# The sums of squares of v fetched through the weights' raw buffers, and split buffers shared by the halves of a lone token block

## The chip, the cores and the metric

The kernel runs on one core of one Trainium2 chip. The core has five engines with a queue each: TensorE (PE in the rows; its weight loads PEld), VectorE (DVE), ScalarE (ACT), GpSimd (POOL) and SyncE (SP), which only issues transfers. DMAs are issued by SyncE, ScalarE and GpSimd and run on the core's 16 DMA engines. The metric is the device time of one execution in microseconds; of several executions the median is told.

## The reference

Three stages on a batch of 4 sequences of 576 tokens. Causal attention with 8 heads of 64 and a decay made from `f`:

```python
log_f = np.log(np.clip(f, 0.0001, 1.0))
cum = np.cumsum(log_f, axis=-1)
decay = cum[:, :, :, None] - cum[:, :, None, :]
scores = np.where(causal, -1000000000.0, scores + decay)
...
return np.matmul(attn, v).astype(np.float32)
```

then a layer norm and an MLP with a residual (512 to 2048 to 512), and a gated layer in which half of the hidden values `v` are normalised and mixed along the sequence by a 576 x 576 matrix:

```python
ch = np.maximum(xn @ w_ch1, 0.0) @ w_ch2
return (x + ch).astype(np.float32)
...
v_s = np.einsum('ts,bsd->btd', w_spatial, v_n) + b_spatial[None, :, None]
gated = u * v_s
return (gated @ w_out).astype(np.float32)
```

## The kernel before, in words

Tokens are handled in nine blocks of 256 columns (`BLOCKS`): blocks 0 and 1 hold the first 128 tokens of two sequences each, 2 and 3 the next 128, 4 to 7 the rest of one sequence each, and block 8 the last 64 tokens of all four. A block first runs through attention (`attention32`, `attention1` or `attention`, by its kind), then the norm, and then the MLP. The MLP takes blocks in groups (`GROUPS`): group 0 is blocks 0 and 1, groups 1 to 5 are one block each (2 to 6), group 6 is blocks 7 and 8.

The work of attention and of the MLP is interleaved by a table of event times in `run`: each event makes one step of a generator issue its instructions, and a scheduling layer then places the instructions in the engines' queues. An engine works off its own queue strictly in order. While group 0 runs through the MLP, the raw 64-bit weights are still fetched, 1 MB for each of 16 slices of the hidden layer, into two `raw` buffers (L474, L475), made into a high and a low single-precision part on ScalarE and VectorE (`narrow`, L463 to L490), and the low part of the second matrix is stored for later groups (L491). At the same time blocks 2 and 3 run through `attention1`.

Attention of blocks 4 to 7 multiplies `v` in two half-precision parts scaled by a power of two, which comes from the sum of squares of `v` in a sequence. `vnorm` makes these sums: it fetches `v`, five times 1 MB (L210, L213), and squares it on ScalarE with an accumulated sum (L211 for four tiles of 128 x 2048, L215 for the last tile in four pieces); one small matmul adds the partitions (L217). Its event time `VN` is 1.6, behind the first part of block 3's attention, and it uses one `vraw` buffer of its own.

The MLP of a group (`mlp`) first splits the normalised block into a high and a low part: for each of four slices of 128 features ScalarE copies `xh` (L543) and VectorE subtracts `xl` (L544). The tiles are 512 columns wide, for two blocks; a lone block uses the first half. There are four buffers of each name. For each of 16 slices j of the hidden layer follow the first layer (12 matmuls into `ph`), `hh` and `hl` on ScalarE and VectorE (L582, L583), and, one slice later, the second layer of slice j - 1 (12 matmuls into `acc`). So between the making of `hh` and the second layer that reads it stand the second layer of the slice before and the first layer of the next. At the end of a group VectorE multiplies the accumulators by the norm's factor into `t` (L598), of which there are three buffers, and GpSimd issues stores of `t` that add to the residual in memory (L600). Group 0 has eight such evictions, a lone block four. L511 is the square in the norm of a block; L380 and L418 are the products of probabilities and `v`; L372 and L281 are the DMA transposes of the probabilities.

Of the kernel before, what the change touches and what calls it, by code (L numbers as in the profile page):

```python
# [6 lines left out]
F32 = mybir.dt.float32  # L7
F32R = mybir.dt.float32r
# [10 lines left out]
P = 128  # L19
B, H, S, D = 4, 8, 576, 64  # L20
DM, DFF, DF2 = 512, 2048, 1024
NK = DM // P
# [3 lines left out]
TOK = 256  # L26
# [7 lines left out]
MB = dict(xT=3, xh=4, hh=2, wl=2, y=2, t=3)  # L34
# [3 lines left out]
RAWB, TMPB, LOB = 2, 2, 4  # L38
# [6 lines left out]
RAMP = 1.5  # L45
# [5 lines left out]
    SPAN.append((SPAN[-1][1], SPAN[-1][1] + (2.25 - E0 - 0.2) / 4))  # L51
SPAN.append((SPAN[-1][1], SPAN[-1][1] + 0.05))
RAWAT = (-1.1, -1.1)
CLEAD, VN = 3, RAMP + 0.1

ORDER = (2, 3, 4, 7, 0, 1, 5, 6)
M2A, M2S = 0.1, 30
# [10 lines left out]
def f32(ap):  # L68
    return ap.bitcast(F32)
# [7 lines left out]
class Kernel:  # L77
# [123 lines left out]

    def vnorm(self):

        nc, at = self.nc, self.at
        ss = self.cst.tile([P, B, 2], F32, name="vss")
        self.vsc = self.cst.tile([P, 2, B], F32, name="vsc")
        for b in range(B + 1):
            t = at.tile([P, 4, DM], F32, tag="vraw", name="vraw", bufs=1)
            if b < B:
                nc.sync.dma_start(out=t, in_=self.v[b, :512].rearrange("(t p) d -> p t d", p=P))  # L210
                nc.scalar.activation(t, t, AF.Square, accum_out=ss[:, b, 0:1])  # L211
            else:
                nc.sync.dma_start(out=t, in_=self.v[:, 512:].rearrange("b p d -> p b d"))  # L213
                for i in range(B):
                    nc.scalar.activation(t[:, i], t[:, i], AF.Square, accum_out=ss[:, i, 1:2])  # L215
        pn = self.bank("s")
        nc.tensor.matmul(pn[:, : 2 * B], lhsT=self.ones, rhs=ss.rearrange("p b u -> p (b u)"), start=True, stop=True)  # L217
        nc.vector.tensor_reduce(out=ss[:, :, 0], in_=pn[:, : 2 * B].rearrange("p (b u) -> p b u", u=2), axis=mybir.AxisListType.X, op=ALU.add)
        self.pow2(ss[:, :, 0], self.vsc)
# [312 lines left out]
    def mlp(self, g, states, y):  # L532
        nc, mo = self.nc, self.mo
        n = len(states)
        xn = [[mo.tile([P, 2 * TOK], F32R, tag=tag, name=tag, bufs=MB["xh"]) for tag in ("xh", "xl")] for _ in range(NK)]

        def split(i):

            x, c = states[i](), slice(i * TOK, (i + 1) * TOK)
            for t, (xh, xl) in enumerate(xn):  # L540
                scale = self.gT[:, t : t + 1]
                with self.tc.high_priority(1):
                    nc.scalar.activation(xh[:, c], x[:, t, :], AF.Copy, scale=scale)  # L543
                    nc.vector.scalar_tensor_tensor(out=xl[:, c], in0=x[:, t, :], scalar=scale, in1=f32(xh[:, c]), op0=ALU.mult, op1=ALU.subtract)  # L544

        acc = self.accs(n * TOK)
        clear, seen = {}, set()

        def second(j, c, hh, hl, wl, last):
            for m in range(NK):  # L550

                bank = m if n > 1 else m // 2
                first = self.mm3(acc[m][:, c], self.wh[:, j, DM + m * P : DM + (m + 1) * P], wl[:, m * P : (m + 1) * P], hh, hl, bank not in clear, last, skip_group_check=True)
                if bank not in clear:
                    clear[bank] = first
                elif (m, c.start, c.stop) not in seen:
                    self.after(first, clear[bank])
                seen.add((m, c.start, c.stop))

        todo = [(j, 0, n) for j in range(NF)]  # L560
        if g == 0:

            todo = [(j, 0, 1) for j in range(SKEW)] + todo[SKEW:] + [(j, 1, 2) for j in range(SKEW)]
        pend, there = None, 0
        for step, (j, i0, i1) in enumerate(todo):
            while there < i1:
                split(there)
                there += 1
            c, W = slice(i0 * TOK, i1 * TOK), (i1 - i0) * TOK
            if g == 0 and i0 == 0:  # L570
                wl = self.w2lo[j]
            else:
                wl = mo.tile([P, DM], F32R, tag="w2l", name="wl", bufs=MB["wl"])
                nc.scalar.dma_start(out=f32(wl), in_=self.w2l_d[j * P : (j + 1) * P, :])
            ph = self.bank("ph")[:, :W]
            for k in range(NK):
                ks = slice(k * P, (k + 1) * P)
                self.mm3(ph, self.wh[:, j, ks], self.w1l[:, j, ks], xn[k][0][:, c], xn[k][1][:, c], k == 0, k == NK - 1)
            hh = mo.tile([P, 2 * TOK], F32R, tag="hh", name="hh", bufs=MB["hh"])[:, :W]
            hl = mo.tile([P, 2 * TOK], F32R, tag="hl", name="hl", bufs=MB["hh"])[:, :W]  # L580
            with self.tc.high_priority(1):
                nc.scalar.activation(hh, ph, AF.Relu)  # L582
                nc.vector.scalar_tensor_tensor(out=hl, in0=ph, scalar=0.0, in1=f32(hh), op0=ALU.max, op1=ALU.subtract)  # L583
            if pend is not None:
                second(*pend)
            pend = (j, c, hh, hl, wl, step == len(todo) - 1)
            yield
        second(*pend)
        c = GROUPS[g][0] * TOK

        W = n * TOK if g == len(GROUPS) - 1 else TOK
        for u in range(n * TOK // W):
            us = slice(u * W, (u + 1) * W)
            for m in range(NK):
                tag, bufs = (("hh", "hl")[m % 2], MB["hh"]) if W > TOK else ("t", MB["t"])
                with self.tc.high_priority(1):
                    t = mo.tile([P, W], F32, tag=tag, name="t", bufs=bufs)
                    nc.vector.tensor_tensor(out=t, in0=y[:, us], in1=acc[m][:, us], op=ALU.mult)  # L598

                nc.gpsimd.dma_start(out=self.x2_d[m * P : (m + 1) * P, c + u * W : c + (u + 1) * W], in_=t, accum_op=ALU.add)  # L600
        yield
# [423 lines left out]
```

## Time and profile before

| | us |
|---|---|
| median of three runs | 867.3 |
| the three runs | 860.18, 867.3, 4240.52 |
| the profiled execution | 855.42 |
| its span | 853.7 |

The profile holds one execution, with the time of each instruction from the span's start. In its rows an idle time stands with what ended it (the releaser), which is inferred from the semaphores: of several it is the one that came last. TensorE's matmuls overlap, so their busy time is less telling than where they stop. The granted clock of TensorE has a mean of 0.98 over the span; the windows give it by stretch.

### The profile page before, as it was taken

Reading aid. Unit: us, or ns where it says so; the run is one execution under the profiler, and the core shown is the slowest. Engines: PE = TensorE matmul, PEld = TensorE weight load, DVE = VectorE, ACT = ScalarE, POOL = GpSimd, SP = SyncE. Lnnn points to the kernel's source line nnn. Section 1 sums busy time; section 2 is a strip of 40 time slices with the busy share of each in tenths; the row PEclk is TensorE's granted clock in tenths of the full one; section 3 lists DMA queues with packets and bytes.
Section 4 is the critical chain, followed back from the end, with each engine's and each line's share of the span. In section 5 each row is a group of like instructions: output and inputs, shape, how many; then the busy total and the mean of one; then the engine's idle time right before and its main releaser. Section 6 shows DMA issues by size and latency. Waiting matters only on the chain.

```text
span 853.7 us, 15349 instructions
## 1 busy us (share of the span) xinstructions
PE 791.1 (93%) x5422; PEld 713.5 (84%) x5422; DVE 540.2 (63%) x1403; ACT 477.5 (56%) x1169; POOL 77.1 (9%) x119
## 2 busy tenths in 40 slices
PE   2888999989999988999899999899999999999998
PEld 1766788878988877889798989878889989999898
DVE  6589997255478878777775873565566743454433
ACT  5787876266668876778775862432424623143220
POOL 3441000030020002001101100200001000000000
PEclk9988999999999997999999999999999999999999
DMA  6587882299689999999999895544545211100101
GB/s 203 158 284 236 246 253 64 71 233 272 167 233 222 249 195 219 206 206 228 198 244 217 209 170 160 158 114 135 168 118 111 63 56 56 57 1 8 49 1 56
DMA packets 181809, 134.30 MB, mean 157 GB/s; under 512 B 108194, under 2 KB 154402, under 8 KB 181732
## 3 DMA queue, kind: packets, MB, share of 16 engines
q1 hardware_dynamic: 160376, 95.09, 45.9%
q10 hardware_dynamic: 16748, 33.51, 13.4%
q0 software_dynamic: 4608, 4.72, 4.0%
q8 instruction: 43, 0.70, 0.3%
q14 instruction: 34, 0.28, 0.1%
HBM read 89.80 MB, written 19.30 MB: 128 GB/s over the span
## 4 chain that ended last, share of the span: by engine, by line
PE 49%; issue 18%; DMA 17%; DVE 7%; ACT 6%; POOL 1%; SPq 1%; ACTq 0%; DVEq 0%; POOLq 0%
PE pb L528 7%; PE pb L527 7%; PE pb L526 7%; DMA PT<-P 4%; PE ph L526 3%; PE ph L527 3%; PE ph L528 3%; PE acc L526 3%; PE s L258 3%; PE acc L527 3%; PE acc L528 3%; DMA x_d<-t 3%; PE av L418 2%; DMA wl<-w2l_d 2%; DMA raw<-in_moe_w_in_dram 2%
## 5 line engine op out<-in xcount | busy, mean ns | idle before, releaser
L526 PE MATMUL ph<-xh,w1l 128*128 128x256 f32 (+1 forms) x456 | 145.0, 320 | 5.3 <-ACT xh L543 4.1
L527 PE MATMUL ph<-xl,wh 128*128 128x256 f32 (+1 forms) x456 | 146.3, 322 | 2.8 <-DVE xl L544 2.8
L528 PE MATMUL ph<-xh,wh 128*128 128x256 f32 (+1 forms) x456 | 144.9, 319 | 0.0
L527 PE MATMUL acc<-hl,wh 128*128 128x256 f32 (+1 forms) x388 | 117.2, 307 | 1.6 <-DVE hl L583 1.5
L528 PE MATMUL acc<-hh,wh 128*128 128x256 f32 (+1 forms) x388 | 115.8, 303 | 0.0
L526 PE MATMUL acc<-hh,wl 128*128 128x256 f32 (+1 forms) x356 | 99.3, 304 | 10.4 <-DMA wl<-w2l_d 5.0
L526 PEld LDWEIGHTS ph<-xh,w1l 128*128 128x128 f32 x456 | 88.7, 195 | 12.6 <-ACT xh L543 5.1
L527 PEld LDWEIGHTS ph<-xl,wh 128*128 128x128 f32 x456 | 89.2, 196 | 9.4 <-DVE xl L544 3.9
L528 PEld LDWEIGHTS ph<-xh,wh 128*128 128x128 f32 x456 | 89.3, 196 | 5.7
L223 ACT ACTIVATE P<-sd,st 128x512 f16<-128x512 f32 (+1 forms) x128 | 71.4, 587 | 26.9 <-DMA PT<-P 20.6
L527 PEld LDWEIGHTS acc<-hl,wh 128*128 128x128 f32 x388 | 74.5, 192 | 6.6 <-DVE hl L583 2.7
L583 DVE SCALAR_TENSOR_TENSOR hl<-ph,hh 128x256 fp32r<-128x256 f32 (+1 forms) x114 | 55.2, 487 | 39.2 <-ACT hh L582 38.9
L526 PEld LDWEIGHTS acc<-hh,wl 128*128 128x128 f32 x356 | 66.3, 193 | 16.1 <-issue 3.3
L279 DVE SCALAR_TENSOR_TENSOR P<-sd,st,P 128x384 f16<-128x384 f32 (+1 forms) x96 | 60.7, 648 | 28.1 <-ACT P L223 27.7
L528 PEld LDWEIGHTS acc<-hh,wh 128*128 128x128 f32 x388 | 74.6, 192 | 3.1
L582 ACT ACTIVATE hh<-ph 128x256 fp32r<-128x256 f32 (+1 forms) x114 | 48.6, 430 | 48.9 <-PE ph L528 42.5
L258 PE MATMUL s<-x 68*128 68x384 f32 (+7 forms) x256 | 58.7, 348 | 7.0 <-DMA x<-decay_d 4.6
L266 ACT ACTIVATE sd<-sd,st 128x384 f32<-128x384 f32 (+2 forms) x80 | 54.6, 683 | 12.6 <-DVE st L262 12.3
L262 DVE CUSTOM_DVE_ANT_0 sd<-s,mask 128x384 f32<-128x384 f32 (+2 forms) x80 | 46.2, 582 | 6.5 <-PE s L258 5.0
L258 PEld LDWEIGHTS s<-x 68*128 68x128 f32 (+3 forms) x256 | 39.8, 185 | 9.4 <-ACT xt L424 3.2
L223 ACT ACTIVATE x<-qk 128x896 fp32r<-128x896 f32 (+1 forms) x64 | 41.5, 698 | 5.0 <-PE s L258 5.0
L418 PE MATMUL av<-PT,vp 128*64 128x320 f16 (+2 forms) x480 | 34.0, 273 | 5.2 <-DMA PT<-P 4.2
(208 smaller groups left out, 1856.6 us busy)
## 6 DMA issues: line engine op xcount, KB each, us to landing
wl<-w2l_d ACTq DMA_DIRECT2D x98, 256.0 KB
raw<-in_moe_w_ch_dram SPq DMA_DIRECT2D x32, 512.0 KB
qk<-in_qk_dram SPq DMA_DIRECT2D x32, 448.0 KB
vraw<-in_v_dram SPq DMA_DIRECT2D x5, 1024.0 KB
vr<-in_v_dram SPq DMA_DIRECT2D x16, 320.0 KB
x_d<-xT SPq DMA_DIRECT2D x9, 512.0 KB
out_dram<-o SPq DMA_DIRECT2D x32, 144.0 KB
w2l_d<-w2lo SPq DMA_DIRECT2D x16, 256.0 KB
```

The lines of the kernel that those rows point to most:

```text
L223: self.nc.scalar.activation(out, in_, AF.Copy, scale=scale)
L258: nc.tensor.matmul(ps[: R * u + R, : c1 - c0], lhsT=x[:, lo - q0 - R * u : hi - q0], rhs=y[:, c0:c1], start=g == 0, stop=g == len(heads[u] ...
L262: nc.vector.tensor_tensor_reduce(out=sd[:M, c0:c1], in0=ps[:M, : c1 - c0], in1=mask, scale=-0.125, scalar=3e38 if n == 0 else st[:M, n - 1 ...
L266: nc.scalar.activation(sd[:M, :N], sd[:M, :N], AF.Exp, bias=st[:M, n : n + 1], scale=-1.0, accum_out=st[:M, 2:3])
L279: nc.vector.scalar_tensor_tensor(out=dl, in0=src, scalar=rs, in1=dh, op0=ALU.mult, op1=ALU.subtract)
L418: nc.tensor.matmul(pav[us, n0:W], lhsT=vp[:kr, vi, kt, us], rhs=heads[u][1][:kr, 2 * kt + pi, n0:W], start=(kt == 0 and (vi, pi) == (0, 1) ...
L526: first = mm(out, lhsT=al, rhs=bh, start=start, stop=False, **kw)
L527: mm(out, lhsT=ah, rhs=bl, start=False, stop=False, **kw)
L528: mm(out, lhsT=ah, rhs=bh, start=False, stop=stop, **kw)
L582: nc.scalar.activation(hh, ph, AF.Relu)
L583: nc.vector.scalar_tensor_tensor(out=hl, in0=ph, scalar=0.0, in1=f32(hh), op0=ALU.max, op1=ALU.subtract)
```

## The change

Two edits. The event time of `vnorm` goes from 1.6 to 1.08, directly behind the making of the last weights, and its five tiles are taken from the pool of the raw weights, under their name `raw`, of which there are two buffers of the same size. In `mlp`, a group of one block takes two tiles of each name instead of four, and uses the first and second halves of each for two slices of features; a group of two blocks does as before.

```diff
-CLEAD, VN = 3, RAMP + 0.1
+CLEAD, VN = 3, RAMP - 0.42
...
     def vnorm(self):
 
-        nc, at = self.nc, self.at
+        nc = self.nc
         ss = self.cst.tile([P, B, 2], F32, name="vss")
         self.vsc = self.cst.tile([P, 2, B], F32, name="vsc")
         for b in range(B + 1):
-            t = at.tile([P, 4, DM], F32, tag="vraw", name="vraw", bufs=1)
+            t = self.st.tile([P, 4, DM], F32, tag="raw", name="vraw", bufs=RAWB)
...
         n = len(states)
-        xn = [[mo.tile([P, 2 * TOK], F32R, tag=tag, name=tag, bufs=MB["xh"]) for tag in ("xh", "xl")] for _ in range(NK)]
+
+        u = 3 - n
+        xn = [[mo.tile([P, 2 * TOK], F32R, tag=tag, name=tag, bufs=MB["xh"]) for tag in ("xh", "xl")] for _ in range(NK // u)]
+        xn = [[t[:, i * TOK : (i + n) * TOK] for t in x] for x in xn for i in range(u)]
```

Behind the edit in `mlp` the lines have numbers three higher (L582 becomes L585, L543 becomes L546).

SyncE's queue at the end of weight making, in the difference of the two orders (`P_1182`, `P_1274`, `P_1411` and `P_1503` are the last four probability tiles of block 2):

```order
-L491 DMA w2l_d<-w2lo 128x512
+L210 DMA vraw<-in_v_dram 128x4x512
+L491 DMA w2l_d<-w2lo 128x512
+L210 DMA vraw<-in_v_dram 128x4x512
 L372 DMA_TRANSPOSE PT<-P_1182 128x8x128
+L210 DMA vraw<-in_v_dram 128x4x512
+L491 DMA w2l_d<-w2lo 128x512
+L210 DMA vraw<-in_v_dram 128x4x512
 L491 DMA w2l_d<-w2lo 128x512
 L372 DMA_TRANSPOSE PT<-P_1274 128x8x128
-L491 DMA w2l_d<-w2lo 128x512
+L213 DMA vraw<-in_v_dram 128x4x512
```

The five fetches stand among the last stores of the weights' low part and ahead of transposes of block 2; before, they stood among the loads and transposes of block 3.

ScalarE's queue in the same place, before:

```order
L381 ACTIVATE xT<-av,vs 128x128
L190 ACTIVATE vp,vq<-vr 128x256
L362 ACTIVATE sd,st<-sd,st 128x256 x2
L363 ACTIVATE st<-st 128x2
L223 ACTIVATE P_1411<-sd,st 128x2x128 x2
L582 ACTIVATE hh<-ph 128x512
L381 ACTIVATE xT<-av,vs 128x128
L198 ACTIVATE vp<-vr,vs 128x256
L582 ACTIVATE hh<-ph 128x512
```

and with the change:

```order
L381 ACTIVATE xT<-av,vs 128x128
L190 ACTIVATE vp,vq<-vr 128x256
L362 ACTIVATE sd,st<-sd,st 128x256 x2
L211 ACTIVATE vraw,vss<-vraw 128x2048
L363 ACTIVATE st<-st 128x2
L585 ACTIVATE hh<-ph 128x512
L223 ACTIVATE P_1411<-sd,st 128x2x128 x2
L215 ACTIVATE vraw,vss<-vraw 128x512 x2
L198 ACTIVATE vp<-vr,vs 128x256
L215 ACTIVATE vraw,vss<-vraw 128x512 x2
L381 ACTIVATE xT<-av,vs 128x128
L585 ACTIVATE hh<-ph 128x512
```

The fourth square of 128 x 2048 and the four short ones stand ahead of the 14th and the 15th `hh` of group 0 now.

ScalarE's queue where block 5 is split for group 4, before; the L511 of that block stands 22 rows ahead of the first of these three copies:

```order
L574 DMA wl<-w2l_d 128x512
L223 ACTIVATE P_5013<-sd,st 128x4x128
L268 ACTIVATE st<-st 128x1
L543 ACTIVATE xh<-xT,gT 128x256 x3
L582 ACTIVATE hh<-ph 128x256
L543 ACTIVATE xh<-xT,gT 128x256
```

and with the change:

```order
L268 ACTIVATE st<-st 128x1
L546 ACTIVATE xh<-xT,gT 128x256 x2
L577 DMA wl<-w2l_d 128x512
L546 ACTIVATE xh<-xT,gT 128x256
L511 ACTIVATE sq<-xT 128x1024
L546 ACTIVATE xh<-xT,gT 128x256
```

The four copies now stand around L511 of their block.

## Rows read from the trace of the kernel before

**Rows 1.** The page's first part: the busy time of TensorE's matmuls and of its weight loads, share of the span and instructions; then VectorE, ScalarE and GpSimd.

```profile
PE 791.1 (93%) x5422; PEld 713.5 (84%) x5422; DVE 540.2 (63%) x1403; ACT 477.5 (56%) x1169; POOL 77.1 (9%) x119
```

**Rows 2.** Windows: one stretch of the span per row. Columns: the stretch in us, its length, the busy time (and instructions) of TensorE, its weight loads, VectorE, ScalarE and GpSimd, the mean granted TensorE clock as a share of 2.4 GHz, the DMA engines' share and the GB/s moved.

```profile
128.00:150.00 22.00, 22.00 (x119) 17.70 (x118) 15.96 (x41) 14.78 (x37) 0.00 (x0) 1.00 0.26 68
150.00:172.00 22.00, 22.00 (x132) 18.38 (x132) 6.26 (x20) 6.19 (x18) 0.00 (x0) 1.00 0.27 73
172.00:196.00 24.00, 18.53 (x134) 17.25 (x132) 14.65 (x51) 14.37 (x44) 8.63 (x10) 0.93 1.08 245
...
240.00:262.00 22.00, 19.23 (x125) 17.29 (x123) 20.03 (x50) 17.63 (x41) 5.83 (x7) 0.92 0.91 232
...
310.00:345.00 35.00, 26.79 (x177) 22.92 (x176) 26.78 (x69) 24.39 (x62) 5.98 (x8) 0.80 0.99 191
...
410.00:455.00 45.00, 39.29 (x339) 36.60 (x336) 32.11 (x91) 31.32 (x84) 3.98 (x6) 1.00 1.07 212
...
540.00:560.00 20.00, 17.01 (x96) 14.34 (x96) 12.60 (x28) 9.74 (x20) 5.65 (x6) 1.00 0.57 139
```

**Rows 3.** Waits from 172 to 196 us: the engine and line that waited, on whom; us in total, times, longest.

```profile
DVE t L598 <- DMA x_d<-t: 6.5, 4, 3.1
...
PE av L380 <- DVE t L518: 0.8, 1, 0.8
```

**Rows 4.** Timeline of the same stretch, VectorE (DVE) and then TensorE (PE): start, us, engine, line, operation, out<-in, size, and in brackets the idle time before it and what ended it.

```profile
184.97 0.42 DVE L598 TENSOR_TENSOR t<-y,s 128x256 f32<-128x256 f32 x1 [2.38 <-DMA x_d<-t]
...
185.88 0.42 DVE L598 TENSOR_TENSOR t<-y,acc 128x256 f32<-128x256 f32 x1 [0.48 <-DMA x_d<-t]
...
186.40 0.55 PE L526 MATMUL acc<-hh,wl 128*128 128x256 f32 x1 [2.38 <-ACT vraw L211]
```

**Rows 5.** GpSimd's stores of t (L600), from issue to landing: the eight of 174 to 200 us, then the four of 240 to 260 us.

```profile
DMA to landing us min/median/max: 4.1/7.7/8.7
...
DMA to landing us min/median/max: 4.1/5.8/6.9
```

**Rows 6.** Timeline, SyncE's queue and ScalarE (ACT): the first fetch of v is issued, and the activation that waits for it.

```profile
173.88 0.38 SPq L210 DMA_DIRECT2D vraw<-in_v_dram  x1
...
184.14 1.91 ACT L211 ACTIVATE vraw<-vraw 128x2048 f32<-128x2048 f32 x1 [2.76 <-DMA vraw<-in_v_dram]
```

**Rows 7.** The chain of waits around the last fetch of v (start, us, what), and the matmul at its end in the timeline of TensorE.

```profile
214.87 5.23 DMA vraw<-in_v_dram
220.12 2.56 ACT vraw L215 x8
...
223.99 0.51 PE L526 MATMUL acc<-hh,wl 128*128 128x256 f32 x2 [0.28 <-ACT hh L582]
```

**Rows 8.** Groups of instructions of ScalarE by line: out<-in xcount | busy us, mean ns of one | idle time before, and what ended it.

```profile
L211 ACT ACTIVATE vraw<-vraw 128x2048 f32<-128x2048 f32 x4 | 7.6, 1911 | 6.8 <-DMA vraw<-in_v_dram 6.8
...
L215 ACT ACTIVATE vraw<-vraw 128x512 f32<-128x512 f32 x4 | 2.5, 619 | 1.6 <-DMA vraw<-in_v_dram 1.6
...
L215 ACT ACTIVATION_READ_ACCUMULATOR vraw<-vraw 128x1 f32 x4 | 0.7, 186 | 0.0
```

**Rows 9.** GB/s that the DMA engines moved in 40 slices of 206 to 216 us, in which the fourth fetch of v runs.

```profile
GB/s 280 250 290 326 271 244 0 2 9 8 10 271 279 352 402 410 393 393 393 393 393 393 393 393 344 410 426 277 273 140 8 7 66 288 154 98 82 328 401 140
```

**Rows 10.** Timeline of the end of weight making and of block 2's last steps: VectorE, ScalarE, SyncE's queue, TensorE.

```profile
126.58 1.22 DVE L466 SCALAR_TENSOR_TENSOR low<-raw,low 128x1024 uint32<-128x1024 uint32 x1 [0.21 <-ACT low L464]
...
133.75 1.13 ACT L463 ACTIVATE tmp<-raw 128x1024 f32<-128x1024 f32 x1
...
148.04 0.60 ACT L582 ACTIVATE hh<-ph 128x512 fp32r<-128x512 f32 x1 [0.51 <-PE ph L528]
...
154.44 0.60 ACT L582 ACTIVATE hh<-ph 128x512 fp32r<-128x512 f32 x1 [3.58 <-PE ph L528]
...
158.23 0.91 ACT L223 ACTIVATE P<-sd,st 128x256 f16<-128x256 f32 x2 [0.23 <-DVE st L364]
...
161.49 0.60 ACT L582 ACTIVATE hh<-ph 128x512 fp32r<-128x512 f32 x1 [2.35 <-PE ph L528]
...
159.73 1.23 SPq L372 DMA_TRANSPOSE PT<-P  x1
...
165.47 0.53 PE L380 MATMUL av<-PT,vp 128*64 128x128 f16 x12
```

**Rows 11.** Timeline of ScalarE: the square of the norm (L511) and the copies to xh (L543) of block 5 (group 4) and of block 7 (group 6, with the first two of its copies).

```profile
397.13 1.06 ACT L511 ACTIVATE sq<-xT 128x1024 f32<-128x1024 f32 x1 [1.05 <-DVE xT L508]
...
406.92 1.30 ACT L543 ACTIVATE xh<-xT,gT 128x256 fp32r<-128x256 f32 x3
...
529.85 1.06 ACT L511 ACTIVATE sq<-xT 128x1024 f32<-128x1024 f32 x1 [1.81 <-DVE xT L508]
...
542.23 0.91 ACT L543 ACTIVATE xh<-xT,gT 128x256 fp32r<-128x256 f32 x2 [1.84 <-PE ph L528]
```

**Rows 12.** Timeline of TensorE: the first matmuls of group 3 and of group 6 that waited for xh or xl.

```profile
331.53 0.39 PE L527 MATMUL ph<-xl,wh 128*128 128x256 f32 x1 [0.75 <-DVE xl L544]
...
334.70 0.51 PE L526 MATMUL ph<-xh,w1l 128*128 128x256 f32 x2 [1.71 <-ACT xh L543]
...
546.67 0.50 PE L527 MATMUL ph<-xl,wh 128*128 128x512 f32 x1 [0.99 <-DVE xl L544]
```

**Rows 13.** Waits from 300 to 345 us, as in rows 3.

```profile
PE s L258 <- DMA x<-decay_d: 3.0, 1, 3.0
```

## The prediction, before any result

> **What bounds the kernel now.** I read the page first, then TensorE by stretch, then its waits. On the page TensorE is busy for 93% of the span [rows 1], so the program ends earlier only where TensorE's idle time or its time at a lower clock shrinks. The windows show where those are [rows 2]. From 128 to 172 us, the late part of group 0's MLP, TensorE is busy for 44.00 of 44 us at full clock: nothing can be won there, and a wait put there counts in full. From 172 to 196 us, where group 0 hands over to group 1, it is busy for 18.53 of 24 us at a mean clock of 0.93. Read a stretch's loss as (length - busy) + (1 - clock) x length, since at the lower of the two clocks (1.2 for 2.4 GHz) matmuls take twice as long: 5.5 + 1.7 = 7.2 us are lost here. In the same way 240 to 262 loses 2.8 + 1.8 = 4.5 us, 310 to 345 loses 8.2 + 7.0 = 15.2, 410 to 455 loses 5.7 and 540 to 560 loses 3.0. All are places where one group of token blocks ends and the next begins.
>
> In the first of them the waits name VectorE: it stands for 6.5 us in four waits until stores of `t` (L598, stored by L600) have landed [rows 3]. The timeline gives the order: VectorE waits 2.38 us, evicts at 184.97 and again at 185.88, and when that second eviction ends, at 186.30, TensorE starts at 186.40 after 2.38 us of idle time [rows 4]. Its row names the activation on `vraw`, which no matmul reads; the bank was what was missing. The stores land late there: 7.7 us in the middle and 8.7 at worst, against 5.8 and 6.9 at the next hand-over, which has no fetch of `v` beside it [rows 5]. The DMA engines are full in that stretch (share 1.08) and a quarter full from 128 to 172 [rows 2].
>
> **The change, part by part.**
>
> *The fetch of v leaves 174 to 223 us.* Five transfers of 1 MB and their squares go. The first took from its issue at 173.88 to the activation's start at 184.14, 10.3 us, in the full stretch [rows 6]; the last one 5.2 us [rows 7]. I take it that without them the stores land as at the next hand-over: 6.9 for 8.7 at worst, 5.8 for 7.7 in the middle, some 1.9 us each. The evictions chain through three `t` buffers, so the first wait of 2.38 falls by 1.9, and the second batch, issued that much earlier and itself 1.9 us faster, lands some 3.8 us sooner. That closes the 2.38, but for half a microsecond that I neglect, and the 0.81 us of idle time ahead of L380 [rows 3, 4]; without the 2.38 the granted clock should stay up, 1.7 us. Term: -4.9 us; bounds 0 (the stores are late for another reason) and -7.2 (the whole loss). The last fetch also held ScalarE up to 223: TensorE was idle 0.28 us for it [rows 7]. Term: -0.3.
>
> The Trainium skill (DMA: Bandwidth & Descriptors, section "Queues, rings and completion order") says that a DMA engine takes turns, packet by packet, between the queue rows that have work. By it a 128 KB store on GpSimd's row is held up by only about its own size in `v`'s bytes, an estimate of 0.5 us at that stretch's 245 GB/s; the wait of 2.38 and the clock would mostly stay, and this term would be near -1 instead of -4.9. The rows differ by 1.9 us, so I go by them.
>
> *The fetch enters 128 to 160 us.* Its five loads now stand among SyncE's stores and transposes, its squares among ScalarE's work. A raw buffer is free once the weights in it are made: VectorE's last read of the last weights but one starts at 126.58, ScalarE's of the last weights at 133.75 [rows 10]. So the loads can go at about 128 and 135, and the next three each behind one activation. Each lands 5.2 us after its issue [rows 7]; the bytes alone need 1.05 MB / 393 GB/s = 2.7 us [rows 9]. With 1.9 + 0.2 us for an activation [rows 8] and ScalarE's other work between, they land near 133, 140, 143, 147 and 152. ScalarE's added work is 7.6 + 2.5 + 0.7 + another 0.7 for the eight accumulator reads = 11.5 us [rows 8], in a stretch where it was busy for 21 of 44 us [rows 2]. What is queued behind it is hh, for which TensorE waits. The hh of 148.04 comes near 152 behind the fourth long square, that of 154.44 near 157.6 behind the four short ones: 4 and 3 us late. A step takes 161.49 - 154.44 = 7.05 us [rows 10], and between making an hh and reading it the program puts the second layer of the step before and the first layer of the next; I count 5.5 of the 7.05 us for these and 1.5 for the attention's matmuls, so both are covered, narrowly. The last probabilities of block 2 slip too: their copy at 158.23 comes near 160.5, their transpose at 159.73 near 162, and their product, which ran at 165.47 [rows 10], 5.7 us behind its transpose, stands a little earlier in TensorE's order than before. TensorE then waits up to 2.7 us; the transpose may land sooner. Term: +1.5; bounds 0 and +22 (third rival).
>
> *Halves share buffers.* A lone block's split takes two of the four buffers of each name, so the next group's copies need not wait until the last first-layer matmul of the group before has read them. For groups 4 to 6 that moves the copies next to L511 of the same block, which they followed by 9.8 us (397 to 407) and 12.4 us (530 to 542) [rows 11]. But TensorE lost little by that. Its idle time behind xl at group 6 is 0.99 us; at group 3 it is 0.75 + 1.71 [rows 12], where ScalarE's new order keeps the four copies as far apart as before. Term: -1.0; bounds 0 and -7 (all three, 3.45, and the 3.5 us that half of that boundary's clock loss is).
>
> *The new order behind 240 us.* The instructions are the same in kind and number, but their order is new everywhere behind the change. Four boundaries lose 4.5, 15.2, 5.7 and 3.0 us [rows 2], 28.4 in all, and so unlike that the order alone seems worth several microseconds at each. I put 0, and as bounds -11 and +11 (a spread of some 5.5 us at each of four, added as if independent).
>
> Sum: -4.9 - 0.3 + 1.5 - 1.0 + 0 = -4.7 against the profiled execution's own 855.4 (span 853.7 and 1.7 around it): 850.7. Of the timed runs one, 4240.5, is no measure; the others, 860.2 and 867.3, stand 5 and 12 us above that execution. I put the median a little above the sum, 852.
>
> **The rivals.**
>
> *Hardly a change* (chance 0.26): three `t` buffers keep the eight evictions of group 0 waiting anyway, or the new order takes back what the hand-over gives. For it: of the 24 us x 245 GB/s = 5.9 MB moved in that stretch [rows 2], the two fetches are only 2.1. Against it: rows 5. Time: 0 to +7 on the profiled execution, 855 to 862. The skill's rule on turns, above, comes to this case.
>
> *Much more* (0.14): with the splits early and out of ScalarE's crowded places, the clock stays up at 240 and at 310 to 345. That gives back 1.8 + 7.0 of clock and half of the 8.2 us of idle time [rows 2], 13 us beyond the sum: 838. For it: those stretches lose most. Against it: TensorE's longest waits there are for a decay load, 3.0 us [rows 13], and for a norm's or `x`'s operands, which the change does not touch.
>
> *Slower: TensorE waits in group 0* (0.10). The place is the four short squares ahead of the 15th hh on ScalarE. If the fetches land as the first one did before, 10.3 us each, the fifth lands near 128 + 5 x 10.3 = 179.5, hh comes 28 us late, 5.5 of them covered: +22, or 871 with the other terms. It decides from a fifth landing behind about 156; each later microsecond counts in full, as TensorE has no idle time there [rows 2]. For it: SyncE issues in order, and block 2's transposes stand behind two, four and five of these loads. Against it: a DMA share of 0.26 where it was 1.08 when the 10.3 was seen. The Trainium skill (the same page and section) says that descriptors of one ring are taken in order; by that a transpose behind a fetch lands later by up to that fetch. No row here has a transpose alone beside a fetch, so this is a reason for the case's chance and not in the sum.
>
> **How the numbers follow.** The forecast's own case, 844 to 857, has 0.50; its time is 852. To hold 8 in 10 I reach from 836, where the second rival ends, to 868, most of the third. A measurement of this kernel tells about 2% from no change, 17 us: 838 and 873 by the profiled execution. Faster by more: the second rival, 0.14. Slower by more: half of the third, 0.05. Within: 0.81.
>
> **What would show it.** Right: no L211 or L215 behind 165 us; group 0's stores landing in under 7 us; from 172 to 196 over 22 us busy at a clock of 1.00; from 128 to 150 still 22 of 22, from 150 to 172 over 20; L543 within 3 us of L511 in groups 4 and 5. Wrong: idle time on TensorE between 140 and 170 that ends with hh or with the product of block 2, or a stretch at the lower clock there; L598 still waiting over 4 us for its stores; or a boundary behind 240 us that gains or loses over 8 us by its order alone.

## The result, and the profile after

The changed kernel took 866.8 us in the median of 20 runs, the kernel before 860.6 us in 20 runs beside it: a ratio of 1.0117, with a 95% interval of 1.0089 to 1.0145. (Some executions of either kernel come out longer, in a slower state; the ratio leaves them out, 2 of the changed kernel's and 11 of the other's, and is so larger than that of the two medians.) The forecast was 852. By the ratio the change made the kernel slower by some 10 us; by the bound of 2% that stands as no change, but the loss is outside the measurement's uncertainty, and its sign is not the forecast's.

The page of the profiled execution after (870.16 us, span 868.4), first part, and three of TensorE's groups (busy us, mean ns | idle us before, and what ended most of it):

```profile
PE 802.9 (92%) x5422; PEld 722.1 (83%) x5422; DVE 541.8 (62%) x1403; ACT 480.3 (55%) x1169; POOL 75.8 (9%) x119
...
L526 PE MATMUL ph<-xh,w1l 128*128 128x256 f32 (+1 forms) x456 | 146.9, 325 | 10.3 <-ACT xh L546 10.3
...
L526 PE MATMUL acc<-hh,wl 128*128 128x256 f32 (+1 forms) x356 | 99.5, 302 | 3.5 <-DMA wl<-w2l_d 1.7
...
L258 PE MATMUL s<-x 68*128 68x384 f32 (+7 forms) x256 | 59.5, 349 | 9.0 <-DMA x<-decay_d 8.1
```

The same three groups on the page of before:

```profile
L526 PE MATMUL ph<-xh,w1l 128*128 128x256 f32 (+1 forms) x456 | 145.0, 320 | 5.3 <-ACT xh L543 4.1
...
L526 PE MATMUL acc<-hh,wl 128*128 128x256 f32 (+1 forms) x356 | 99.3, 304 | 10.4 <-DMA wl<-w2l_d 5.0
...
L258 PE MATMUL s<-x 68*128 68x384 f32 (+7 forms) x256 | 58.7, 348 | 7.0 <-DMA x<-decay_d 4.6
```

The work is the same; the waits are others: longer for xh and for a decay load, shorter for wl. Added up, TensorE's idle time is only 2.9 us longer than on the page of before (65.5 of 868.4 us for 62.6 of 853.7). The other 11.8 us between the two spans are busy time, 802.9 for 791.1 us with the same 5422 matmuls; the mean granted clock is 0.965 in this execution and was 0.980 in that of before. (Lines behind L535 are three higher after the change.) The windows of after, for the stretches of [rows 2]:

```profile
128.00:150.00 22.00, 22.00 (x118) 17.78 (x118) 16.32 (x38) 18.34 (x35) 0.00 (x0) 1.00 0.80 255
150.00:172.00 22.00, 21.44 (x131) 17.23 (x130) 7.50 (x24) 12.18 (x35) 0.00 (x0) 1.00 0.54 129
172.00:196.00 24.00, 21.43 (x155) 19.64 (x154) 15.50 (x54) 14.13 (x45) 9.19 (x10) 0.94 0.94 172
240.00:262.00 22.00, 19.17 (x136) 18.17 (x135) 16.32 (x39) 13.96 (x31) 5.63 (x6) 0.92 0.80 218
310.00:345.00 35.00, 26.14 (x176) 23.16 (x176) 27.55 (x75) 25.05 (x64) 6.45 (x8) 0.83 1.15 234
410.00:455.00 45.00, 42.12 (x339) 38.50 (x338) 33.31 (x88) 32.69 (x82) 4.50 (x8) 0.92 0.97 209
540.00:560.00 20.00, 20.00 (x154) 19.36 (x153) 11.50 (x27) 8.01 (x17) 4.46 (x5) 1.00 0.52 163
```

The stretch that the change was expected to help is better: from 172 to 196 us TensorE loses 2.6 us idle and 1.4 to the clock, 4.0 for 7.2. Behind it the windows go both ways: 540 to 560 gains 3.0 us, 410 to 455 gains 2.8 us of busy time and loses 3.6 at the lower clock. The new idle time for xh stands for the most part where group 3 begins. SyncE's store of the raw block (L863), VectorE, ScalarE and TensorE in the timeline there:

```profile
325.85 0.62 SPq L863 DMA_DIRECT2D x_d<-xT  x1
...
332.37 1.42 DVE L508 TENSOR_TENSOR xT<-xT,av 128x256 f32<-128x256 f32 x4 [2.60 <-DMA x_d<-xT]
...
332.82 0.51 ACT L546 ACTIVATE xh<-xT,gT 128x256 fp32r<-128x256 f32 x1 [2.31 <-DVE xT L508]
...
337.83 0.49 ACT L546 ACTIVATE xh<-xT,gT 128x256 fp32r<-128x256 f32 x1
...
333.38 0.79 PE L526 MATMUL ph<-xh,w1l 128*128 128x256 f32 x2 [2.76 <-ACT xh L546]
...
338.37 0.80 PE L526 MATMUL ph<-xh,w1l 128*128 128x256 f32 x2 [2.39 <-ACT xh L546]
```

The norm writes in place, so VectorE waits until the store issued at 325.85 has read the block; xh follows, and its second copy stands behind other work of ScalarE. It is the obvious suspect. The experiments show that such waits need not cost the kernel its time.

### The profile page after: what moved, and what is told of

Read it like the earlier page. It is cut to its first block, busy times and chain, and to the rows that moved or that the text cites. A ratio compares the mean times of both kernels' runs of the same rounds, so it can differ in the third digit from the quotient of the medians.

```text
span 868.4 us, 15319 instructions
## 1 busy us (share of the span) xinstructions
PE 802.9 (92%) x5422; PEld 722.1 (83%) x5422; DVE 541.8 (62%) x1403; ACT 480.3 (55%) x1169; POOL 75.8 (9%) x119
## 4 chain that ended last, share of the span: by engine, by line
PE 48%; DMA 20%; issue 15%; DVE 8%; ACT 5%; SPq 2%; POOL 1%; ACTq 0%; DVEq 0%; POOLq 0%
PE pb L527 7%; PE pb L528 7%; PE pb L526 7%; DMA PT<-P 6%; PE ph L527 3%; PE ph L526 3%; PE acc L526 3%; PE ph L528 3%; PE acc L527 3%; PE acc L528 3%; PE av L418 2%; PE s L258 2%; DMA x_d<-t 2%; DMA raw<-in_moe_w_in_dram 2%; DMA wl<-w2l_d 2%
## 5 line engine op out<-in xcount | busy, mean ns | idle before, releaser
L526 PE MATMUL ph<-xh,w1l 128*128 128x256 f32 (+1 forms) x456 | 146.9, 325 | 10.3 <-ACT xh L546 10.3
L585 ACT ACTIVATE hh<-ph 128x256 fp32r<-128x256 f32 (+1 forms) x114 | 48.7, 430 | 54.8 <-PE ph L528 53.2
L279 DVE SCALAR_TENSOR_TENSOR P<-sd,st,P 128x384 f16<-128x384 f32 (+1 forms) x96 | 58.5, 625 | 26.0 <-ACT P L223 25.6
L223 ACT ACTIVATE x<-qk 64x320 fp32r<-64x320 f32 (+1 forms) x64 | 42.0, 698 | 0.5 <-PE s L258 0.2
```

Of the source, the lines that this page charges most:

```text
L223: self.nc.scalar.activation(out, in_, AF.Copy, scale=scale)
L279: nc.vector.scalar_tensor_tensor(out=dl, in0=src, scalar=rs, in1=dh, op0=ALU.mult, op1=ALU.subtract)
L526: first = mm(out, lhsT=al, rhs=bh, start=start, stop=False, **kw)
```

## The experiments

Three theories to begin with. A: sharing buffers between halves makes TensorE wait for xh. B: the edits are as good as forecast, but any edit ahead of 240 us gives the program another order behind it, and that order is worse. C: the fetch among group 0 costs the time.

**One edit at a time, and no edit at all.** The first kernel has only the first two hunks of the change, the second only the third, and the third is this:

```diff
-CLEAD, VN = 3, RAMP + 0.1
+CLEAD, VN = 3, RAMP + 0.05
```

Fetch alone:

> Only the fetch of v is moved (VN = RAMP - 0.42, its tiles from the raw weights' buffers); each lone block's split keeps four buffers of each name. The changed kernel is at 1.0117 of before: against the forecast it lost its time where groups 2 and 3 begin (TensorE waits 1.9, 2.8 and 2.4 us for xh there) and by more half-clock stretches. Theory A (the shared halves cause the waits for xh): this one has none of them and keeps what the hand-over of group 0 gives, ratio 0.990 to 0.998. Theory B (whatever moves an instruction ahead of 240 us gives the program a new order behind it, and the order decides what the starts of groups cost): the ratio is anywhere from 0.987 to 1.013, and the losses stand at other starts than in the changed kernel. Theory C (the fetch among group 0 costs the time itself): 1.008 to 1.015, with idle time from 128 to 172 us.

Measured: 1.0042 (1.0004 to 1.0079), which neither A nor C gave and B allows.

Halves alone:

> Only the shared halves; the fetch of v stays where it was. Theory A: the waits for xh at the starts of groups 2 and 3 are as long as in the changed kernel (some 7 us together), the 2.4 us at 184 us are there as before, ratio 1.010 to 1.022. Theory B: the ratio is anywhere from 0.987 to 1.013 and the waits at the starts are new ones. Theory C: as before or a little faster, 0.992 to 1.000.

Measured: 1.0119 (1.0062 to 1.0176), as A had it; B allows that too.

No edit but a number:

> The kernel before with one number changed: VN = RAMP + 0.05 for RAMP + 0.1, so v is fetched a little earlier behind the hand-over, into its own buffer. No buffer changes and no work; TensorE's order changes from that place to the end. Theory B: its time differs from before by 3 us or more, either way, and TensorE's idle time at the starts of groups 2 to 6 is spread in another way. Theories A and C: within 0.3 % of before (0.997 to 1.003), since neither the halves nor the place of the fetch among group 0 is touched.

Measured: 1.0158 (1.0103 to 1.0212), more than the whole change loses. It touches no buffer, and v is fetched by the same instructions a few steps earlier. Only theory B allowed for a change there, in either direction. It does not yet say what part of the change's own loss is order.

**The edits without the new order.** A table holds each engine to the order of the kernel before, by edges that set an order and make no wait:

```diff
+    def pin(self):
+        for code in TABLE.values():
...
+                if last is not None:
+                    self.tc.add_manual_dep(ins[at], last.name, nosync, reason="order")
+                last = ins[at]
```

For the moved fetch, its five loads and eight squares stand behind the neighbours that they have in the changed kernel, its matmul and four VectorE instructions ahead of the first of block 3; all else is in the old order, and the score banks rotate as before. In the traces the halves alone run in the order of the kernel before on every engine, instruction for instruction. The kernel before with such a table and no edit was not run, so what the table does by itself is not measured apart from the halves (0.9974, below).

> The shared halves alone, with every engine's instructions held in the order of the kernel before by a table. All that is left of the edit is that the copies xh and xl of groups 1 to 6 no longer wait for TensorE's last reads of the buffers. Theory A (the shared halves themselves cost the time): some 1.01, as in the run with the halves and an order of their own (1.0119). Theory B (the order that came with them does): as before, 0.996 to 1.002, since a wait is only taken away.

Measured: 0.9974 (0.9934 to 1.0014).

> The fetch of v alone is moved to where the changed kernel has it (five loads on SyncE, eight squares on ScalarE, one matmul, four small VectorE instructions), and every other instruction of all engines is held in the order of the kernel before by a table. Theory B: this is the prediction's first two terms without its fourth, -4.9 - 0.3 + 1.5 = -3.7 us, ratio 0.992 to 1.000; TensorE's 2.4 us of idle time where group 0 hands over to group 1 are gone. Theory C (the move itself costs): 1.003 or more, with idle time ahead of hh or of block 2's last product from 128 to 172 us.

Measured: 0.9953 (0.9913 to 0.9993).

> Both edits of the change, all other instructions in the order of the kernel before. Theory B: the forecast's sum, -4.7 us, ratio 0.990 to 1.000, some 15 us under the changed kernel, which is the same work in another order. Theory A: as the changed kernel, 1.008 to 1.015.

Measured: 0.9951 (0.9918 to 0.9984), or -4.2 us of 860; the forecast's sum was -4.7. The same instructions in the changed kernel's own order make 1.0117. So the order alone costs 1.7%, 14 us (some 13 us between the two kernels' own medians, which were not taken side by side). Theory A falls with the first of the three, C with the second. VectorE's wait for stores of t in this last kernel from 172 to 206 us, and its stores' landing from 174 to 205 us (lines are 11 higher than in the changed kernel: L612 is the eviction):

```profile
DVE t L612 <- DMA x_d<-t: 2.2, 1, 2.2
```

```profile
DMA to landing us min/median/max: 3.2/4.2/5.2
```

**Where the new order costs.** The orders of the two kernels differ only in short pieces between which each engine has done the same instructions in both, so they can be spliced. Four kernels have both edits, the old order, and the changed kernel's order in one stretch:

```diff
-order[e] = old[e]
+order[e] = old[e][:i] + new[e][i:j] + old[e][j:]   # e7: to 236 us, e8: 236 to 400, e9: 400 to 632, e10: from 632
```

> Both edits; up to 236 us of the program the engines' order is that of the changed kernel, behind it that of the kernel before. The run with both edits wholly in the old order was 0.9951; between its profiled execution and the changed kernel's, idle time and half of the half-clock time add 3.4 us up to the start of group 2 (242 us). If the losses of the new order simply add up place by place: ratio 0.9951 + 3.4/860 = 0.999. If a hand-over's loss only shows with the order ahead of it as well (rival): this one still 0.995.

Measured: 0.9990 (0.9951 to 1.0029).

> Both edits; the changed kernel's order from 236 to 400 us only (groups 2 and 3, with the waits of 1.9, 2.8 and 2.4 us for xh), the old order elsewhere. By place: the profiles' difference here is -1.6 us (group 2 better, group 3 worse), so 0.993 to 0.997. If the waits for xh are what the changed kernel lost: 0.9951 + 7/860 = 1.003.

Measured: 0.9975 (0.9946 to 1.0005).

> Both edits; the changed kernel's order from 400 to 632 us only (groups 4, 5 and 6). By place: +6.2 us by the profiles, ratio 1.002. Rival: the loss there is handed on from group 3 and does not come without it, 0.995.

Measured: 1.0110 (1.0061 to 1.0159).

> Both edits; the changed kernel's order behind 632 us only, which is the second MLP alone. By place: +5.9 us by the profiles (a wait of 3.3 us for vt at its first block, where the kernel before waits 1.0 us, and 6.8 us at half clock behind it), ratio 1.002. If the clock falls there by chance only: +2.3 us, 0.998.

Measured: 0.9969 (0.9938 to 0.9999).

TensorE's waits from 236 to 400 us in the kernel with the new order there, and then in the changed kernel:

```profile
PE ph L537 <- ACT xh L557: 6.5, 3, 2.9
PE s L269 <- DMA x<-decay_d: 5.1, 2, 3.0
```

```profile
PE ph L526 <- ACT xh L546: 7.0, 3, 2.8
PE s L258 <- DMA x<-decay_d: 7.0, 4, 2.7
```

The suspect of the profile is there almost whole, 6.5 of 7.0 us for xh, and that kernel is not slower than before. What the new order loses at group 3 it has won before: in that kernel's profiled execution the time from the first matmul of group 2 to that of group 3 is 85.0 us, for 91.5 with both edits in the old order, and from there to group 4 84.9 for 80.8. The one loss clear of noise comes with the stretch from 400 to 632 us, 1.6%. The four differences to 0.9951 add up to 2.4%, over the 1.7% of the whole; each has an interval of 0.3 to 0.5% to either side, and a splice costs something itself. Right behind the end of the stretch from 400 to 632 us the kernel with the new order there waits 3.4 us for hh. The same wait stands in another kernel with that splice (the one with late copies, below); these are its rows, the second one the window with the lower clock, and then the same place in the changed kernel:

```profile
641.53 1.22 PE L537 MATMUL acc<-hh,wl 128*128 128x512 f32 x2 [3.80 <-ACT hh L596]
...
640.60:647.40 6.80, 5.45 (x12) 3.86 (x13) 4.22 (x7) 1.97 (x4) 0.86 (x1) 0.50 0.22 77
```

```profile
643.38 0.73 PE L526 MATMUL acc<-hh,wl 128*128 128x512 f32 x2 [0.37 <-ACT hh L585]
```

The changed kernel waits 0.4 us there and the old order not at all, so up to 7 us (3.8 idle and up to 3.4 at the lower clock) of the 14 us that the stretch seems to lose by itself belong to the splice. Without them the four places would add up to about the whole.

**What in that stretch.** A shorter piece, the copies xh and xl of groups 4 and 5 moved alone, the new order with those copies moved back, and the reverse splice:

```diff
# e11
+order[e] = old to 400 us + new to 485 us + old
# e12: old order, but on ScalarE and VectorE xh and xl of groups 4 and 5 go
-behind sq by 11 and 17 us
+next to sq
# e13: the order of e9, with the same copies moved the other way
# e14
+order[e] = new to 400 us + old to 632 us + new
```

> Both edits; the changed kernel's order from 400 to 485 us only (end of group 3, group 4). The new order from 400 to 632 us made 1.011. Theory D (the loss comes where block 6's attention meets group 4: its transposed probabilities are late and TensorE waits for them, four waits of 1.1 to 1.6 us between 433 and 457 us in that run): most of it is here, 1.004 to 1.011. Theory E (it is spread over the boundaries of groups 4, 5 and 6 alike): a third of it, 1.000.

Measured: 1.0062 (1.0024 to 1.0099), two thirds of what the longer piece loses. But the longest wait of its profiled execution from 400 to 500 us, 3.2 of 6.4 us for transposed probabilities, stands behind the end of the splice, and so does one for wl:

```profile
490.47 0.35 PE L537 MATMUL acc<-hh,wl 128*128 128x256 f32 x1 [1.37 <-DMA wl<-w2l_d]
494.00 0.48 PE L429 MATMUL av<-PT,vp 128*64 128x320 f16 x1 [3.17 <-DMA PT<-P]
```

So how much of it is the piece's own stays open, and with it theory D against E.

> Both edits, old order, but the four copies xh and the four xl of groups 4 and 5 stand right behind sq of the same block, as the change makes possible, 11 and 17 us ahead of where the old order has them. Theory F (the early copies push the attention's softmax on ScalarE and VectorE back, and with it the transposes): 1.000 to 1.011. Theory G (the order of the attention's own work is what costs): 0.995, as without.

Measured: 0.9957 (0.9916 to 0.9997). The early copies cost nothing.

> Both edits, the changed kernel's order from 400 to 632 us, but the copies of groups 4 and 5 moved back to 11 and 17 us behind sq. Theory F: the loss goes, 0.995 to 1.000. Theory G: it stays, 1.007 to 1.012.

Measured: 1.0077 (1.0044 to 1.0109). The loss stays, or most of it, with the wait at the splice's end in it.

> Both edits, the changed kernel's order everywhere but from 400 to 632 us, where the old one stands. If that stretch holds the loss: 1.0117 - 0.0159 = 0.996, or with the three small differences of the other stretches added up (0.0039 + 0.0024 + 0.0018 over 0.9951) 1.003 at most. If the loss comes from anywhere the order is new: 1.008.

Measured: 0.9996 (0.9962 to 1.0029). With the old order in that one stretch the changed kernel is as fast as the kernel before, and 1.2 of the 1.7% are gone. So most of the loss needs the new order in that stretch. That the stretch alone is enough for it is not shown, since up to half of its own loss is the splice's.

TensorE's groups from 390 to 650 us, first with both edits in the old order, then with the new order from 400 to 632 us and late copies (busy us, mean ns | idle us and what ended it):

```profile
L537 PE MATMUL acc<-hh,wl 128*128 128x256 f32 (+1 forms) x188 | 52.9, 309 | 2.8 <-DVE t L612 1.8 <-DMA wl<-w2l_d 0.9
L269 PE MATMUL s<-x 68*128 68x384 f32 (+3 forms) x112 | 23.6, 332 | 0.0
L429 PE MATMUL av<-PT,vp 128*64 128x320 f16 (+2 forms) x261 | 17.8, 269 | 4.0 <-ACT sd L277 2.5 <-DMA PT<-P 1.0 <-issue 0.5
```

```profile
L537 PE MATMUL acc<-hh,wl 128*128 128x256 f32 (+1 forms) x184 | 51.7, 310 | 8.1 <-DMA wl<-w2l_d 4.2 <-ACT hh L596 3.8
L269 PE MATMUL s<-x 68*128 68x384 f32 (+3 forms) x112 | 24.7, 337 | 2.5 <-DMA x<-decay_d 1.5 <-ACT P L234 1.1
L429 PE MATMUL av<-PT,vp 128*64 128x320 f16 (+2 forms) x240 | 17.2, 271 | 4.1 <-DMA PT<-P 3.8 <-PE s L269 0.3
```

In these three groups idle time is 6.8 us in the old order and 14.7 in the new, and waits for transfers (wl, PT, a decay load) are 9.5 us of it for 1.9; the 3.8 us for hh are those at the splice's end. But the changed kernel's own profiled execution has only some 8 us of waits in that stretch, for 10 in the kernel before and 7.5 in the old order, so this is how one such order loses, not a proof for the other. Which instruction's place does it is not settled. The new order on one computing engine alone, or on all but one, was not tried, since the engines would wait for each other in a ring. On SyncE alone it could be:

```diff
-order["SP"] = old["SP"]
+order["SP"] = old["SP"][:275] + new["SP"][275:354] + old["SP"][354:]
```

> Both edits, old order on TensorE, VectorE, ScalarE and GpSimd; only SyncE issues its loads, stores and transposes from 400 to 632 us in the changed kernel's order. If the loss is SyncE's: 1.005 to 1.011. If it is in the order of the computing engines: 0.994 to 0.998.

Measured: 1.0002 (0.9971 to 1.0032). That is between the two expectations, 0.5% over 0.9951 with some 0.45% to either side: part of the loss may be SyncE's, and the rest needs the other engines' order.

**A good order before, or a bad one after?** Three more orders, made by another event time of `vnorm`:

```diff
# e16, the kernel before
-VN = RAMP + 0.1
+VN = RAMP - 0.1
# e17 and e18, the changed kernel
-VN = RAMP - 0.42
+VN = RAMP - 0.5   # e18: RAMP - 0.6
```

> The kernel before with VN = RAMP - 0.1: no edit of buffers, another order behind the hand-over of group 0. If the order of the kernel before is an unusually good one: slower, 1.005 to 1.016, as with VN = RAMP + 0.05. If the orders of the changed kernel and of that run were unusually bad: 0.995 to 1.003.

Measured: 1.0216 (1.0176 to 1.0257).

> The changed kernel with VN = RAMP - 0.5 for RAMP - 0.42: both edits, a third order. If the old order is unusually good: 1.004 to 1.016. If the changed kernel's order is unusually bad: 0.995 to 1.000, the forecast's value.

Measured: 1.0102 (1.0055 to 1.0150).

> The changed kernel with VN = RAMP - 0.6: both edits, a fourth order. As for the run before: 1.004 to 1.016, or 0.995 to 1.000.

Measured: 1.0172 (1.0123 to 1.0221).

Every kernel whose order the scheduling layer made anew, beside the kernel before:

| edits | ratios | mean |
|---|---|---|
| none, VN + 0.05 and - 0.1 | 1.0158, 1.0216 | 1.019 |
| fetch alone; halves alone | 1.0042; 1.0119 | |
| both, VN - 0.42, - 0.5, - 0.6 | 1.0117, 1.0102, 1.0172 | 1.013 |

All seven are slower than before. Two of them are more than a new order: at - 0.5 and - 0.6 the event stands ahead of the last weights, which are then fetched up to 149.5 us instead of 124.1, and at - 0.6 TensorE waits 1.2 us for hh at 156.5 and 1.5 us for transposed probabilities at 164.0, in group 0 itself. The order of the kernel before is a good one, and the changed kernel's is an ordinary one among these. Between the means of the first row and the last lie 0.6%, in the direction and of the size that the fixed order gave for the edits (0.5%), though two and three draws are few. The orders lose at different places. On the page of the order at - 0.1 without edits, and of that at - 0.6 with both, the groups of matmuls with the most idle time are

```profile
L418 PE MATMUL av<-PT,vp 128*64 128x320 f16 (+2 forms) x480 | 35.5, 278 | 13.0 <-DMA PT<-P 9.6
```

```profile
L526 PE MATMUL acc<-hh,wl 128*128 128x256 f32 (+1 forms) x356 | 98.3, 303 | 10.0 <-DMA wl<-w2l_d 8.1
```

where the changed kernel has 10.3 us for xh. The version that beats both is the one with both edits in the old order, 0.9951; the fetch alone in that order is as good.

## Why the prediction was wrong

**The step that failed is the fourth term, "The new order behind 240 us": 0, with bounds of -11 and +11.** Measured by both edits with and without it, it is 1.0117 - 0.9951 = 0.0166, 14 us. The spread was sized from four boundaries' losses [rows 2] and was only a little too small. The centre was wrong: I took a new order to be as likely better as worse. Seven of seven draws came out worse, by 0.4 to 2.2%. Most of it needs the new order from 400 to 632 us; which instruction's place makes it stays open. That the range of 836 to 868 still holds the median of 866.8 is luck: its upper part stands for the third rival, which did not happen. Unlike boundaries in one kernel say how far orders can differ, but not where the one at hand stands among them. The rival "hardly a change" had the right words, that the new order takes back what the hand-over gives, and a price of 0 to +7 for what was 14 less 4.

**The fetch leaves 174 to 223 us: -4.9 - 0.3.** The part with the waits came, the part with the clock did not. The squares of v and the fetch's issues after the change (first and last start), the stores of t from 170 to 205 us, and the waits from 172 to 200 us:

```profile
L210 SPq DMA_DIRECT2D vraw<-in_v_dram x4: 368/390/416, 129.7 to 144.8; - x4
L211 ACT ACTIVATE vraw<-vraw x4: 1902/1912/1918, 136.7 to 151.4; 128x2048 f32<-128x2048 f32 x4
...
L215 ACT ACTIVATE vraw<-vraw x4: 614/615/631, 156.7 to 159.0; 128x512 f32<-128x512 f32 x4
```

```profile
DMA to landing us min/median/max: 3.0/5.2/5.6
```

```profile
DVE t L601 <- DMA x_d<-t: 2.3, 2, 1.5
...
PE av L380 <- DMA PT<-P: 2.8, 1, 2.8
```

The stores land in 5.6 us at worst, better than the 6.9 that I took from the next hand-over [rows 5]; VectorE waits 2.3 us for them instead of 6.5 [rows 3], and the idle time of 2.38 us is gone. In its place the changed order has 2.8 us for transposed probabilities; in the old order, with the fetch alone, TensorE's gaps there are 0.63 and 0.93 us. The clock did not stay up as I had it: 0.94 from 172 to 196 us, not 1.00. Nor did it with both edits in the old order, whose windows are these; then that of before from 196 to 240 us:

```profile
172.00:196.00 24.00, 21.26 (x157) 19.77 (x156) 15.63 (x53) 13.57 (x44) 8.51 (x10) 0.97 0.98 200
196.00:240.00 44.00, 43.75 (x379) 41.42 (x378) 18.96 (x73) 20.75 (x68) 0.72 (x1) 0.94 0.55 126
```

```profile
196.00:240.00 44.00, 43.62 (x389) 41.03 (x390) 19.48 (x77) 27.64 (x82) 0.58 (x1) 1.00 0.88 213
```

The fall comes later and lasts longer there, 3.4 us of clock over both stretches for 1.7 before. From the first matmul of group 1 to that of group 2 this kernel takes 66.3 us for 68.9, so in these two executions the two terms are 2.6 us and not 5.2. That all terms but the fourth together came to -4.2 us for -4.7 is therefore in part luck, and the interval is 3 us to either side.

The Trainium skill (DMA: Bandwidth & Descriptors, "Queues, rings and completion order") has an engine take turns between queue rows, from which I estimated that the stores would keep most of their delay and this term would be near -1. The traces side with the rows here: without the fetch beside them the worst store lands in 5.6 us for 8.7, and in 5.2 in the old order.

**The fetch enters 128 to 160 us: +1.5.** It came later than I had it, and cost less. The fifth load, issued at 149.90, let the short squares start at 156.7, where I had 152; the hh behind them ran at 159.82 instead of 157.6. TensorE did not wait for either hh. The last matmul of this hh's first layer, the hh, and the first matmul that reads it:

```profile
155.90 0.40 PE L528 MATMUL ph<-xh,wh 128*128 128x512 f32 x1
...
159.82 0.58 ACT L585 ACTIVATE hh<-ph 128x512 fp32r<-128x512 f32 x1
...
163.43 0.39 PE L526 MATMUL acc<-hh,w2lo 128*128 128x512 f32 x1
```

The last product of block 2 waited, as forecast, but 0.56 us and not 2.7:

```profile
167.75 0.53 PE L380 MATMUL av<-PT,vp 128*64 128x128 f16 x12 [0.56 <-DMA PT<-P]
```

(0.84 us in the old order). So the third rival, four short squares ahead of hh, fell, though the fifth landing was at its point of 156: in this execution the first layer ended at 156.3, so that the hh was 3.5 us late, and 7.1 us lay between that end and the reading.

**Halves share buffers: -1.0.** In the old order 0.9974, or -2 with 3 us either way: neither its size nor its sign is resolved. The copies did move next to the squares, as forecast, now within 1.5 us of L511 in groups 4 and 5:

```profile
405.86 1.29 ACT L546 ACTIVATE xh<-xT,gT 128x256 fp32r<-128x256 f32 x3
407.06 1.05 ACT L511 ACTIVATE sq<-xT 128x1024 f32<-128x1024 f32 x1
...
469.79 0.91 ACT L546 ACTIVATE xh<-xT,gT 128x256 fp32r<-128x256 f32 x2
470.60 1.04 ACT L511 ACTIVATE sq<-xT 128x1024 f32<-128x1024 f32 x1
```

That gave nothing (0.9957 with the early copies, 0.9951 without), and TensorE had hardly waited for them before [rows 12].

**Much more** (splits early, clock up at 310 to 345 us) fell: the clock there is 0.83 for 0.80, and TensorE waits longer for xh.

The prediction's list of signs named "a boundary behind 240 us that gains or loses over 8 us by its order alone". No boundary does so by idle time and clock in the windows: in the stretch that holds most of the loss, 410 to 455 us loses 6.5 us for 5.7 before, and 540 to 560 nothing for 3.0. Only the splices pointed to it.

## What to carry to other kernels

Where a scheduling layer orders the program, an edit is two changes: the edit, and a new draw of the order. Here the edit was worth -4 us and the draw +14. The kernel here stood on a good order and lost by each of seven new ones, so where that may be so, price the new order as a loss, of the size that a change of one number without effect shows, and judge an edit with the order held fixed; then keep the order. And do not take the longest new wait of a profile for the loss: here a kernel with 6.5 of its 7 us was not slower, and a splice of the orders, stretch by stretch, is what pointed to the place. A splice makes waits of its own at its ends (3.8 us here), so read its profile there, and run the reverse splice too.

## What was not expected of the hardware

Up to half of what the order costs is TensorE's clock. Over the timed runs the granted clock has a median of 0.970 in the changed kernel and 0.977 with both edits in the old order: (1 - 0.970) x 865 = 26 us against (1 - 0.977) x 852.4 = 20, 6 of the 12.6 us between their medians (866.7 and 854.1). That is an upper bound, since it counts TensorE's idle time at the lower clock as if it were work; what the clock costs was not measured apart. All orders that lose 1% or more have a median of 0.965 to 0.972, all that are faster than before one of 0.975 to 0.978. An idle time that an order adds can come with a loss of clock: in the changed kernel the 3.3 us for vt that end at 679.45 stand beside 6.8 us at half the clock, in 5.0 of which TensorE is busy, some 2.5 us more.

```profile
677.60:684.40 6.80, 4.95 (x20) 4.95 (x21) 4.39 (x9) 6.09 (x15) 0.00 (x0) 0.50 0.24 73
```

It does not always: with both edits in the old order 2.5 us of idle time end at 424.38, and the clock is 1.00 from 420 to 440 us. And one profiled execution doesn't show the clock of the median: the changed kernel's had 0.965.
